# Attention and a dense block on one core: a list-scheduled order over named buffers, row-tiled scores, pooled V by matmul, q and k pooled before their transposes

## Chip, cores, metric

The kernel runs on one core of one Trainium2 chip. The metric is device time in microseconds (us), the median of several runs. The kernel before takes 449.98 us (median of 3 runs, 449.43 to 450.81).

Engine names as the profile has them: PE is TensorE, PEld its weight loads (these overlap PE), DVE VectorE, ACT ScalarE, POOL GpSimd, SP the queue that issues loads and stores.

## The reference

```python
# q, k, v: [8 batches, 8 heads, 576, 64]; w_in: [512, 2048]; w_out: [2048, 512]
q_d, k_d, v_d = (t.reshape(B, H, 144, 4, D).mean(axis=3) for t in (q, k, v))
out_d = softmax(scale * q_d @ k_d.T) @ v_d               # 144 pooled positions
out_up = np.repeat(out_d, 4, axis=2)
mask = np.abs(pos[:, None] - pos[None, :]) < 4           # a band of 7 keys
out_local = softmax(where(mask, scale * q @ k.T, -1e9)) @ v
x = (out_up + out_local) -> [4608, 512]                  # token major
h = x @ w_in
return (h - np.tanh(h)) @ w_out                          # [4608, 512]
```

There are two parts. Attention works on 32 pairs of heads, four pairs to a batch. The dense part, two matrix products, works on nine blocks of 512 tokens, and each block needs all four pairs of the batches that its tokens come from.

## The kernel before

A pair's q and k come in as tokens by features. DVE reorders them, PE transposes them into PSUM, ACT evicts them into `qk`. DVE then copies the keys into `kz`, whose other head's rows are zero, so that a full 128-row matmul gives the scores of one head. POOL pools q and k from the evicted transposes.

```python
def a_T(p):
    ...                                     # 9 transposes, 3 evictions to qk
    for hh in range(2):                     # zero-padded keys, one per head
        nc.vector.tensor_copy(out=kz[r, hh], in_=win)
    nc.gpsimd.tensor_tensor(out=tmp, in0=v2[:, :, :, 0], in1=v2[:, :, :, 1], op=ALU.add)
    nc.gpsimd.tensor_tensor(out=qd[:, 0], in0=t2[:, 0, :, 0], in1=t2[:, 0, :, 1], op=ALU.add)
    for hh in range(2):
        nc.gpsimd.tensor_tensor(out=kd[r, :, 64 * hh:64 * hh + 48], ...)
    nc.gpsimd.tensor_scalar_mul(qd[:, 1], qd[:, 0], 1.0 / 16.0)

def a_S(p, hh):                             # scores of one head
    for t in range(NT):
        nc.tensor.matmul(ps[...], kz[:, hh, t, :], qk[:, QW * t:QW * t + NQ[t]], ...)
    for i, m in enumerate(ms):
        nc.tensor.matmul(ps[...], kd[:, m, :], qd, ...)
    ...                                     # exp on ACT, mask on DVE
```

V is loaded twice: once in overlapping windows of 128 tokens (`vst`), once grouped by four tokens (`vg`), from which POOL pools it.

```python
def prep_v(hb):                             # four heads
    nc.gpsimd.tensor_copy(out=vw3[hb % 3][:, :, :, 0:64], in_=vst[hb])
    nc.gpsimd.tensor_tensor(out=tmp, in0=vg[:, :, :, 0:128], in1=vg[:, :, :, 128:256], op=ALU.add)
    for i in range(2):
        nc.gpsimd.tensor_tensor(out=vd[r, ...], in0=tmp[r, :, :, 0:64], in1=tmp[r, :, :, 64:128], op=ALU.add)
```

The order of the program is written by hand. `pump(n)` puts up to n quads (four matmuls of 128x512, 0.87 us) of dense work between the steps, if their batches are done.

```python
for p in range(NPAIR):
    ...                                     # loads
    a_T(p + 1); pump(1)
    a_O(p); pump(2)                         # outputs, normalisation
    a_S(p + 1, 0); pump(1)
    a_X(p); pump(1)                         # transpose back to xT
    a_S(p + 1, 1)
    a_reorder(p + 2); prep_v(...); load_v(...)
    pump(3)
while quads:
    quads.pop(0)[1]()                       # the dense work that is left
```

The softmax here doesn't subtract the row's maximum and nothing guards it: scores larger than these inputs give would overflow.

Of the kernel before, what the change touches and what calls it, by code (L numbers as in the profile page):

```python
# [10 lines left out]
ALU = mybir.AluOpType  # L11
PSUM = bass.MemoryType.PSUM


@with_exitstack
def kernel(
# [14 lines left out]
    NPAIR = B * NP  # L31
    G = S // 4
# [10 lines left out]
    work = ctx.enter_context(tc.tile_pool(name="work", bufs=2))  # L43
    moe = ctx.enter_context(tc.tile_pool(name="moe", bufs=2))
    ps_a = ctx.enter_context(tc.tile_pool(name="ps_a", bufs=1, space=PSUM))
    ps_m = ctx.enter_context(tc.tile_pool(name="ps_m", bufs=4, space=PSUM))

    def fixed(name, shape, dt):
        return const.tile(shape, dt, name=name, tag=name)

    ident = fixed("ident", [128, 128], BF16)
    mask = fixed("mask", [128, 576], BF16)
# [3 lines left out]
    qk2 = [fixed(f"qk{i}", [128, 1192], BF16) for i in range(2)]  # L56
    kz2 = [fixed(f"kz{i}", [128, 2, NT, 128], BF16) for i in range(2)]
    kd2 = [fixed(f"kd{i}", [128, 3, 128], BF16) for i in range(2)]
    vw3 = [fixed(f"vw{i}", [128, 4, NT, 65], BF16) for i in range(3)]
    vg2 = [fixed(f"vg{i}", [128, 2, 3, 256], FP32) for i in range(2)]  # L60
    vd3 = [fixed(f"vd{i}", [128, 2, 3, 130], BF16) for i in range(3)]


    def emit_ident():
        nc.gpsimd.memset(ident, 0.0)
        nc.gpsimd.affine_select(
            out=ident, in_=ident, compare_op=ALU.not_equal, fill=1.0,
            base=0, pattern=[[-1, 128]], channel_multiplier=1,
        )

    def emit_zeros(i):
        nc.vector.memset(qk2[i], 0.0)
        nc.vector.memset(kz2[i], 0.0)
        nc.vector.memset(kd2[i], 0.0)

    def emit_vzeros(i):
        if i < 2:
            nc.vector.memset(vg2[i], 0.0)
        nc.vector.memset(vd3[i], 0.0)
        nc.vector.memset(vd3[i][0:48, :, :, 64:65], 4.0)  # L80
        nc.vector.memset(vd3[i][64:112, :, :, 129:130], 4.0)
        nc.vector.memset(vw3[i][:, :, :, 64:65], 1.0)

    def emit_mask():

        nc.gpsimd.memset(mask, 1.0)
        m4 = mask[:, 0:480].rearrange("p (t c) -> p t c", c=QW)
        for part, pat in ((m4, [[0, 4], [1, QW]]),
                          (mask[:, 480:576], [[1, 96]])):
            neg = [[-s, n] for s, n in pat]  # L90
            nc.gpsimd.affine_select(
                out=part, in_=part, compare_op=ALU.is_ge, fill=0.0,
                base=-1, pattern=neg, channel_multiplier=1)
            nc.gpsimd.affine_select(
                out=part, in_=part, compare_op=ALU.is_ge, fill=0.0,
                base=7, pattern=pat, channel_multiplier=-1)
        nc.gpsimd.affine_select(
            out=mask[:, 0:QW], in_=mask[:, 0:QW], compare_op=ALU.is_ge,
            fill=0.0, base=-4, pattern=[[0, QW]], channel_multiplier=1)
        nc.gpsimd.affine_select(  # L100
# [4 lines left out]
    qkn, tails, vst = {}, {}, {}  # L105

    def load_qk(hb):
        b, h0 = hb // 2, 4 * (hb % 2)
        t = work.tile([128, 2, 4, 256], BF16, name="qkn", tag="qkn", bufs=3)
        qkn[hb] = t  # L110
        for i, src in enumerate((q, k)):
            nc.gpsimd.dma_start(
                out=t[:, i],
                in_=src[b, h0:h0 + 4, 0:512, :].rearrange(
                    "h (g a) d -> g h (a d)", a=4))
        if hb % 2 == 0:
            tl = work.tile([128, H * D], BF16, name="tl", tag="tl")
            tails[b] = tl
            for i, src in enumerate((q, k)):
                nc.gpsimd.dma_start(  # L120
                    out=tl[64 * i:64 * i + 64, :].rearrange(
                        "p (h d) -> p h d", d=D),
                    in_=src[b, :, 512:576, :].rearrange("h p d -> p h d"))

    def load_v(hb):
        b, h0 = hb // 2, 4 * (hb % 2)
        t = work.tile([128, 4, NT, 64], FP32, name="vst", tag="vst")
        vst[hb] = t
        for i in range(4):
            h = h0 + i  # L130
            base = v[b, h]

            def win(tok, n, nt):
                return bass.AP(tensor=base.tensor, offset=base.offset + tok * D,
                               ap=[[D, n], [QW * D, nt], [1, D]])
            if b == 0 and h == 0:
                nc.vector.memset(t[0:32, i, 0, :], 0.0)
                nc.sync.dma_start(out=t[4:128, i, 0, :], in_=v[b, h, 0:124, :])
                nc.sync.dma_start(out=t[:, i, 1:5, :], in_=win(QW - 4, 128, 4))
            elif b == B - 1 and h == H - 1:  # L140
                nc.vector.memset(t[96:128, i, 4, :], 0.0)
                nc.sync.dma_start(out=t[0:100, i, 4, :], in_=v[b, h, 476:576, :])
                nc.sync.dma_start(out=t[:, i, 0:4, :], in_=win(-4, 128, 4))
            else:
                nc.sync.dma_start(out=t[:, i], in_=win(-4, 128, 5))
        vg = vg2[hb % 2]
        for i in range(4):
            nc.sync.dma_start(
                out=vg[64 * (i % 2):64 * (i % 2) + 48, i // 2],
                in_=v[b, h0 + i].rearrange("(m g a) d -> g m (a d)", m=3, a=4))  # L150

    def prep_v(hb):
        nc.gpsimd.tensor_copy(out=vw3[hb % 3][:, :, :, 0:64], in_=vst[hb])
        vg, vd = vg2[hb % 2], vd3[hb % 3]
        tmp = work.tile([128, 2, 3, 128], FP32, name="vtmp", tag="vtmp", bufs=1)
        nc.gpsimd.tensor_tensor(out=tmp, in0=vg[:, :, :, 0:128],
                                in1=vg[:, :, :, 128:256], op=ALU.add)
        for i in range(2):
            r = slice(64 * i, 64 * i + 48)
            nc.gpsimd.tensor_tensor(  # L160
                out=vd[r, :, :, 65 * i:65 * i + 64], in0=tmp[r, :, :, 0:64],
                in1=tmp[r, :, :, 64:128], op=ALU.add)


    st = {}

    def a_reorder(p):
        src = qkn[p // 2]
        qr = work.tile([128, 2, 4, 128], BF16, name="qr", tag="qr")
        st[p] = {"qr": qr}  # L170
        h = 2 * (p % 2)
        for i in range(2):
            nc.vector.tensor_copy(  # L173
                out=qr[:, i].rearrange("p a (h d) -> p h a d", d=D),
                in_=src[:, i, h:h + 2, :].rearrange("p h (a d) -> p h a d", d=D))

    def a_T(p):
        qr, tl = st[p]["qr"], tails[p // 4]
        j = p % 4
        ps = ps_a.tile([128, 2, 1024], BF16, name="ps_t", tag="ts")  # L180
        for i in range(2):
            for a in range(4):
                nc.tensor.transpose(  # L183
                    ps[:, 0, 512 * i + 128 * a:512 * i + 128 * a + 128],
                    qr[:, i, a, :], ident)
        nc.tensor.transpose(ps[:, 1, 0:128], tl[:, 128 * j:128 * j + 128], ident)  # L186
        qk = qk2[p % 2]
        full = bass.AP(tensor=qk.tensor, offset=qk.offset,
                       ap=[qk.ap[0], [KOFF, 2], [1, 576]])
        for i in range(2):  # L190
            nc.scalar.copy(  # L191
                out=full[:, i, 0:512].rearrange("p (g a) -> p g a", a=4),
                in_=ps[:, 0, 512 * i:512 * i + 512].rearrange(
                    "p (a g) -> p g a", a=4))
        nc.scalar.copy(  # L195
            out=full[:, :, 512:576],
            in_=ps[:, 1, 0:128].rearrange("p (i c) -> p i c", i=2))

        kz = kz2[p % 2]
        for hh in range(2):  # L200
            r = slice(64 * hh, 64 * hh + 64)
            kk = qk[r, :]
            win = bass.AP(tensor=kk.tensor, offset=kk.offset + KOFF - 4,
                          ap=[kk.ap[0], [QW, NT], [1, 128]])
            nc.vector.tensor_copy(out=kz[r, hh], in_=win)  # L205

        tmp = work.tile([128, 2, 288], BF16, name="tmp", tag="tmp")
        v2 = full.rearrange("p i (g a) -> p i g a", a=2)
        qd = work.tile([128, 2, G], BF16, name="qd", tag="qd")
        with nc.allow_low_precision("pooled q and k"):  # L210
            nc.gpsimd.tensor_tensor(out=tmp, in0=v2[:, :, :, 0],  # L211
                                    in1=v2[:, :, :, 1], op=ALU.add)
            t2 = tmp.rearrange("p i (g a) -> p i g a", a=2)
            nc.gpsimd.tensor_tensor(out=qd[:, 0], in0=t2[:, 0, :, 0],  # L214
# [222 lines left out]
```

## Time and profile before

| what | value |
|---|---|
| time, span of the profiled run | 449.98 us, 448.2 us |
| PE, DVE, ACT, POOL busy | 77%, 61%, 46%, 50% |
| first dense matmul starts (timeline) | 72.9 us |
| last transpose back of attention starts | 371.7 us |
| from there to the end: dense work alone | 219 ns per matmul |

The page of the kernel before: the busy line, the span in 40 slices of 11.2 us (each digit tenths busy), and the chain of work that ended last.

```profile
span 448.2 us, 6961 instructions
PE 344.2 (77%) x2550; PEld 198.6 (44%) x2592; DVE 271.2 (61%) x486; ACT 206.8 (46%) x373; POOL 222.1 (50%) x293
...
PE   1034447864888888888888888888888889999996
...
DMA  9999998530563656484919290929023010101111
...
PE 47%; POOL 23%; DVE 15%; issue 6%; ACT 6%; DMA 2%; SPq 2%; POOLq 0%; ACTq 0%
```

PE is busy at most four tenths in the first six slices, some eight tenths in the body, and full at the end. POOL holds 23% of the chain though it is busy only half the time, so some of PE's waits are for it. The first six slices have the DMA engines at nine tenths.

The timeline of the kernel before, a piece of the start (start us, duration us, engine, line, operation; in brackets the idle time before it and what ended it):

```profile
53.04 1.15 POOL L211 TENSOR_TENSOR tmp<-qk_79 128x576 bf16<-128x576 bf16 x1 [3.31 <-ACT qk_79 L195]
53.53 0.66 PE L231 MATMUL ps_s_436<-qk_79,kz_81 128*128 128x120 bf16 x5 [0.83 <-DVE kz_81 L205]
54.27 0.42 POOL L214 TENSOR_TENSOR qd<-tmp 128x144 bf16<-128x144 bf16 x1
54.65 0.91 POOL L220 TENSOR_TENSOR kd_83<-tmp 64x144 bf16<-64x144 bf16 x2
...
55.66 0.56 POOL L223 TENSOR_SCALAR qd<-qd 128x144 bf16<-128x144 bf16 x1
56.27 0.40 PE L236 MATMUL ps_s_436<-qd,kd_83 128*128 128x144 bf16 x2 [2.08 <-POOL qd L223]
...
61.85 1.03 PE L183 MATMUL ps_t<-ident,qr 128*128 128x128 bf16 x8 [3.44 <-DVE qr L173]
```

The pooled scores (L236) wait 2.08 us for four POOL operations that could begin only when the transposes were evicted; the next pair's transposes start 8.3 us after the first scores. In the body the same waits recur, 1.3 us each, and a pair takes 11 us.

### The profile page before, as it was taken

What the parts mean: (1) busy time and instruction counts of PE and PEld (TensorE: products, weight loads), DVE (VectorE), ACT (ScalarE), POOL (GpSimd) and SP (SyncE); (2) the same over time, 40 slices, a digit from 0 to 9 for tenths busy, and PEclk for the clock granted to TensorE, in tenths of its full rate; (3) what the DMA queues carried; (4) which work ended last, traced back from release to release, by engine and by line L of the source; (5) the groups of instructions that cost most, each with busy time, mean ns of one, the idle gap of its engine ahead of it and who ended that gap; (6) DMA issues with size and microseconds to landing.
All of it is one profiled execution on the core that took longest, in us unless ns stands there. A gap on an engine that the chain in (4) does not pass through costs nothing.

```text
span 448.2 us, 6961 instructions
## 1 busy us (share of the span) xinstructions
PE 344.2 (77%) x2550; PEld 198.6 (44%) x2592; DVE 271.2 (61%) x486; ACT 206.8 (46%) x373; POOL 222.1 (50%) x293
## 2 busy tenths in 40 slices
PE   1034447864888888888888888888888889999996
PEld 0023335543545454545454444545454554444442
DVE  6025464966676777777777767676767665343420
ACT  1122224752455555555555555555555543444421
POOL 7478686646665755666465747574727220000000
PEclk9999999985799999999999999999999999999999
DMA  9999998530563656484919290929023010101111
GB/s 126 213 193 198 169 200 104 112 48 0 60 141 66 147 73 131 77 160 57 171 35 177 41 182 26 179 40 181 25 75 95 22 41 25 47 25 47 44 52 70
DMA packets 86993, 43.44 MB, mean 97 GB/s; under 512 B 52655, under 2 KB 82351, under 8 KB 86959
## 3 DMA queue, kind: packets, MB, share of 16 engines
q1 hardware_dynamic: 57390, 29.36, 27.4%
q0 software_dynamic: 29568, 13.64, 24.4%
q8 instruction: 20, 0.33, 0.3%
q14 instruction: 15, 0.11, 0.1%
HBM read 47.18 MB, written 9.44 MB: 126 GB/s over the span
## 4 chain that ended last, share of the span: by engine, by line
PE 47%; POOL 23%; DVE 15%; issue 6%; ACT 6%; DMA 2%; SPq 2%; POOLq 0%; ACTq 0%
PE ps_h L308 17%; PE ps_y L322 17%; DVE E L244 9%; POOL tmp L211 8%; PE ps_t L183 4%; POOL qd L223 4%; ACT E L242 4%; POOL qd L214 3%; POOL kd_82 L220 3%; POOL kd_83 L220 3%; PE ps_o L262 2%; PE ps_o L255 2%; DMA vg_87<-in_v_dram 2%; DVE gT L313 1%; DVE qr L173 1%
## 5 line engine op out<-in xcount | busy, mean ns | idle before, releaser
L322 PE MATMUL ps_y<-w_out_sb,gT 128*128 128x512 bf16 x547 | 139.5, 379 | 1.5
L312 ACT ACTIVATE u<-ps_h 128x512 f32<-128x512 f32 x144 | 86.1, 598 | 101.9 <-PE ps_h L308 100.8
L313 DVE TENSOR_TENSOR gT<-ps_h,u 128x512 bf16<-128x512 f32 x144 | 98.6, 687 | 50.0 <-ACT u L312 49.2
L244 DVE TENSOR_TENSOR E<-E,mask 128x576 bf16<-128x576 bf16 x64 | 59.4, 928 | 49.5 <-ACT E L242 49.4
L308 PEld LDWEIGHTS <-w_in_sb 128*128 128x128 bf16 x576 | 54.4, 99 | 55.9 <-issue 2.2
L322 PEld LDWEIGHTS <-gT 128*128 128x128 bf16 x576 | 53.7, 98 | 51.5
L211 POOL TENSOR_TENSOR tmp<-qk_79 128x576 bf16<-128x576 bf16 x16 | 18.3, 1146 | 78.6 <-PE ps_o L262 60.7
L308 PE MATMUL ps_h<-xT_74,w_in_sb 128*128 128x512 bf16 x144 | 55.3, 384 | 0.1
L308 PE MATMUL ps_h<-xT_73,w_in_sb 128*128 128x512 bf16 x142 | 54.5, 384 | 0.9 <-issue 0.4
L308 PE MATMUL ps_h<-xT_75,w_in_sb 128*128 128x512 bf16 x143 | 54.9, 384 | 0.0
L308 PE MATMUL ps_h<-xT_72,w_in_sb 128*128 128x512 bf16 x134 | 51.1, 382 | 0.1
L183 PE MATMUL ps_t<-ident,qr 128*128 128x128 bf16 x256 | 23.0, 242 | 32.8 <-DVE qr L173 32.8
L211 POOL TENSOR_TENSOR tmp<-qk_78 128x576 bf16<-128x576 bf16 x16 | 18.3, 1144 | 40.7 <-PE ps_o L262 31.9
L183 PEld LDWEIGHTS <-qr 128*128 128x128 bf16 x256 | 18.0, 108 | 43.0 <-DVE qr L173 40.1
L205 DVE COPY kz_81<-qk_79 64x640 bf16<-64x640 bf16 x32 | 15.5, 486 | 27.7 <-ACT qk_79 L195 27.2
L205 DVE COPY kz_80<-qk_78 64x640 bf16<-64x640 bf16 x32 | 15.5, 485 | 26.6 <-ACT qk_78 L195 26.1
L327 ACT COPY y<-ps_y 128x512 f32<-128x512 f32 x36 | 21.1, 585 | 20.0 <-PE ps_y L322 20.0
L191 ACT COPY qk_78<-ps_t 128x512 bf16<-128x512 bf16 x32 | 17.2, 591 | 24.9 <-PE ps_t L186 24.9
L269 DVE TENSOR_TENSOR ln<-ps_o,r 128x640 bf16<-128x640 f32 x32 | 26.4, 824 | 1.1
L191 ACT COPY qk_79<-ps_t 128x512 bf16<-128x512 bf16 x32 | 17.2, 591 | 8.1 <-PE ps_t L186 8.1
L236 PEld LDWEIGHTS <-kd_82 128*128 128x128 bf16 x48 | 4.9, 102 | 35.6 <-POOL kd_82 L220 26.6
L223 POOL TENSOR_SCALAR qd<-qd 128x144 bf16<-128x144 bf16 x32 | 18.1, 566 | 2.9
(272 smaller groups left out, 514.2 us busy)
## 6 DMA issues: line engine op xcount, KB each, us to landing
vst<-in_v_dram SPq DMA_DIRECT2D x62, 160.0 KB, 3.3
out_dram<-y SPq DMA_DIRECT2D x36, 256.0 KB, 2.0
vg_87<-in_v_dram SPq DMA_DIRECT2D x32, 144.0 KB, 4.2
vg_88<-in_v_dram SPq DMA_DIRECT2D x32, 144.0 KB, 4.3
qkn<-in_q_dram POOLq DMA_DIRECT2D x16, 256.0 KB, 4.8
qkn<-in_k_dram POOLq DMA_DIRECT2D x16, 256.0 KB, 5.6
w_in_sb<-in_moe_w_in_dram POOLq DMA_DIRECT2D x4, 512.0 KB, 8.4
w_out_sb<-in_moe_w_out_dram POOLq DMA_DIRECT2D x4, 512.0 KB, 8.5
```

Of the source, the lines that this page charges most:

```text
L183: nc.tensor.transpose(ps[:, 0, 512 * i + 128 * a:512 * i + 128 * a + 128], qr[:, i, a, :], ident)
L191: nc.scalar.copy(out=full[:, i, 0:512].rearrange("p (g a) -> p g a", a=4), in_=ps[:, 0, 512 * i:512 * i + 512].rearrange("p (a g) -> p g a ...
L205: nc.vector.tensor_copy(out=kz[r, hh], in_=win)
L211: nc.gpsimd.tensor_tensor(out=tmp, in0=v2[:, :, :, 0], in1=v2[:, :, :, 1], op=ALU.add)
L220: nc.gpsimd.tensor_tensor(out=kd[r, :, 64 * hh:64 * hh + 48], in0=t3[:, :, :, 0], in1=t3[:, :, :, 1], op=ALU.add)
L223: nc.gpsimd.tensor_scalar_mul(qd[:, 1], qd[:, 0], 1.0 / 16.0)
L244: nc.vector.tensor_tensor(out=E[:, hh, 0:576], in0=E[:, hh, 0:576], in1=mask, op=ALU.mult)
L269: nc.vector.tensor_tensor(out=ln[:, 0:5, :].rearrange("p t (h d) -> p h t d", d=D), in0=blocks[:, :, 0:5, 0:64], in1=r[:, :, 0:5].unsqueez ...
L308: nc.tensor.matmul(ps, w_in_sb[:, dc, fc * 128:(fc + 1) * 128], xT[dc][:, kb * 512:kb * 512 + 512], start=(dc == 0), stop=(dc == N_DC - 1))
L312: nc.scalar.activation(out=u, in_=ps, func=AF.Tanh)
L313: nc.vector.tensor_tensor(out=gTs[kb][:, fc, :], in0=ps, in1=u, op=ALU.subtract)
L322: nc.tensor.matmul(ps, gTs[kb][:, fc, ts * 128:ts * 128 + 128], w_out_sb[:, fc, :], start=(fc == 0), stop=(fc == N_FF - 1))
```

## The change

There are four parts. (1) The hand-written order goes. Each step is given to a small list scheduler with its engine, an assumed duration in ns, the names of the buffers it reads and writes, and a priority; it simulates the engines and emits in order of start. (2) Scores are row-tiled: the two heads sit in rows 0 to 63 and 64 to 127, each matmul uses its 64 rows, and the `kz` copies go. (3) V is loaded once, and six matmuls with a 0/1 matrix sum its groups of four. (4) q and k are pooled on POOL before the transposes, straight from the loaded layout, and matmuls with the identity transpose the sums. The first pairs also alternate between two sets of PSUM banks.

The diff holds smaller changes too. The main ones: q and k are loaded by pair (128 KB a load) and no longer by four heads (256 KB). The scores of a pair come in two groups over both heads, and only the second holds pooled scores; before, the first head's group held some already and waited for them. The exps, the masks and the normalisation are regrouped to match: masks of 960 and 192 columns for two of 576, one normalisation of 896 for 640 and 256. And the second product of the first dense block follows its first product at once, so that 32 quads and not 16 can be done before the second batch is.

```diff
+class Program:
+    def op(self, eng, ns, fn, reads=(), writes=(), pri=0): ...   # dependencies by name
+    def order(self): ...          # list schedule: earliest engine, lowest priority
 ...
-            nc.vector.tensor_copy(out=kz[r, hh], in_=win)
 ...
+        def score(t, hh, c):
+            rows = slice(64 * hh, 64 * hh + 64)
+            k0 = KOFF + QW * t - 4
+            T.matmul(sc[:, c:c + NQ[t]], qk[s][rows, k0:k0 + 128],
+                     qk[s][rows, QW * t:QW * t + NQ[t]], start=True, stop=True)
 ...
+            for t in range(NT):                                  # pooled V
+                T.matmul(pv[:, 0, :], pick[:, t, :], vw[w][:, :, t, 0:64],
+                         start=(t == 0), stop=(t == NT - 1))
 ...
+                GP.tensor_tensor(out=sm1, in0=src[:, :, :, 0:128],
+                                 in1=src[:, :, :, 128:256], op=ALU.add)
 ...
+        if p < NP and p % 2 == 1:
+            ps, po, ts, ox = ps_ts1, ps_ox1, ["ts1"], ["ox1"]
 ...
-    for p in range(NPAIR):
-        ...  a_T, pump, a_O, pump, a_S, ...
+    P.emit()
```

## The prediction

> **What bounds the kernel now** (span 448.2 us). Two things, in turn.
> (1) Start: the timeline shows the first dense matmul at 72.9 us. Until then pairs of heads run one after another, PE under 5 of each 10 us. The chain of waits runs through POOL: V pooling until 22 us, then per pair tmp 1.15, qd 0.43, kd 0.91, qd 0.57 us while the scores wait.
> (2) 110 to 370 us: one pair per 11 us (21.95 us per two, by the starts of tmp in the chain), PE busy 83 to 87%. The order is fixed: eight dense quads (4 matmuls of 128x512, 0.87 us) per pair, and waits for qd recur (1.3 us). The remaining dense work runs alone from 370 us at 219 ns per matmul, PE 99% busy.
>
> PE's own work by instruction starts: dense 1152 x 0.219 = 252 us, attention about 2.25 us per pair. From 72.9 us that is 252 + 28 x 2.25 = 315 us, but the last matmul ends at 444.5: 57 us of gaps.
>
> **What changes, per pair (estimates from durations in the trace).**
> - POOL: tmp/qd/kd (3.0 us) and half of V's cast, vtmp and vd (2.6) become two adds (1.6) and a cast (0.65). POOL leaves the chain; half-size loads add 0.8 us of issue.
> - DVE: two kz copies (0.97 us) go; kd out of PSUM (0.27) comes. Masks: 0.66 + 0.26 us uncontended (576 columns took 459 ns median, 928 mean, up to 2.1 us beside POOL's adds and casts).
> - ACT: qd (0.28) and a V eviction (0.25) are added; about 4.0 us.
> - PE: pooling transposes and V matmuls add 0.5 us; row tiling saves 0.3 if the two heads' scores overlap. The Trainium skill, "TensorEngine Tiling (Array Packing)", Key Properties, says changing tiling mode drains TensorE; four changes per pair, which no run here shows yet. I count 2.5 us plus drains.
> - DMA: the second V load (9.4 MB) goes. This matters only in the first 63 us, where the queues are saturated (near 200 GB/s).
>
> **Where it counts.** Pooled q/k no longer wait for evicted transposes, and early pairs alternate between two PSUM sets. Chain per pair: transposes 0.9, evictions 1.7, scores and exps 2.8, output to xT 4 us, two deep. I expect the first dense matmul at 43 us (gain 30), limited by loads and POOL's order.
> After it PE-bound: 252 + 28 x 2.5 = 322 us. The emitted order has about 6 quads per pair, and stretches around pairs 7-8 and 11-12 with no dense work left, where PE must wait. With these, drains, and DVE and ACT over 80% busy I add 25 us of gaps. The end (copy, store) is 3.7 us as now; timing is 1.8 us above the span.
> 43 + 322 + 25 + 5.5 = 395; attention started before 43 us gives back 4.
>
> **Predicted: 391 us, 80% range 375 to 409. Faster 0.97, same 0.02, slower 0.01.**
>
> **What would show it.** First dense matmul at 38 to 48 us; PE over 88% busy from there; attention over by 275 us, then dense alone for 105 us; POOL busy about 140 us and out of the chain; the two heads' score matmuls starting within a few ns.
>
> **What would make it wrong.** w_out late (saturated queues until 65 us) with PE's order fixed; drains over 0.2 us each; a static order built on durations shorter than measured (tanh 598 ns, subtract 687 ns), so that PE stalls each pair; masks still blocked by POOL.

## The result, and the profile after

The changed kernel is correct and takes 393.9 us (median of 4 runs, 393.53 to 394.27); the kernel before took 450.01 us in the same rounds. The ratio is 0.8752, with a 95% interval of 0.8736 to 0.8768. A ratio here is the mean time of one kernel's runs over that of the other's of the same rounds, so not quite the ratio of the medians quoted. Executions over 1.5% slower than the fastest of the same kernel are left out of the means.

The page of the changed kernel, the same lines (slices of 9.8 us):

```profile
span 392.6 us, 7296 instructions
PE 348.9 (89%) x2835; PEld 191.5 (49%) x2880; DVE 228.9 (58%) x417; ACT 221.8 (56%) x421; POOL 151.0 (38%) x203
...
PE   1466798976996899999999999999999999999996
...
PEclk9997599998999799999999999999999999999999
DMA  9699993466759648568554400000010010101012
...
PE 80%; ACT 8%; DVE 8%; issue 2%; DMA 2%; POOL 1%; ACTq 0%; DVEq 0%; POOLq 0%
```

PE does the same amount of busy time, 349 against 344 us, in a span that is 56 us shorter. POOL has left the chain. The granted clock (PEclk) dips in the fourth, fifth, tenth and fourteenth slices, in which PE was six to eight tenths busy. The first dense matmul starts at 43.1 us (before 72.9), the last transpose back at 287.6 us (before 371.7), and dense work is alone for 101 us at the end. PE's remaining idle time sits early, as the windows of the changed kernel show (stretch: its length, then busy us of each engine, the granted PE clock, the DMA share and GB/s):

```profile
42.90:100.00 57.10, 48.39 (x384) 25.71 (x390) 31.32 (x58) 31.95 (x60) 31.15 (x39) 0.93 0.76 122
100.00:150.00 50.00, 44.94 (x475) 28.12 (x481) 40.45 (x77) 36.19 (x74) 34.78 (x45) 0.93 0.65 106
150.00:288.00 138.00, 135.57 (x1306) 77.20 (x1327) 99.59 (x184) 97.11 (x191) 49.55 (x62) 1.00 0.37 71
288.00:388.90 100.90, 100.36 (x458) 45.49 (x465) 35.93 (x52) 39.53 (x68) 0.00 (x0) 1.00 0.11 42
```

From 43 to 388.9 us PE is idle for 16.7 us of 346, and 13.8 us of that lie before 150 us. The kernel before had lost much more in the same parts; its windows:

```profile
72.90:110.00 37.10, 26.33 (x217) 16.65 (x218) 28.16 (x51) 19.50 (x37) 22.79 (x29) 0.83 0.35 53
110.00:150.00 40.00, 32.88 (x261) 19.82 (x267) 27.05 (x48) 20.86 (x38) 24.51 (x31) 0.90 0.47 80
150.00:370.00 220.00, 187.32 (x1525) 108.86 (x1549) 157.76 (x282) 120.47 (x220) 123.01 (x160) 1.00 0.50 98
370.00:444.60 74.60, 74.08 (x344) 33.73 (x348) 25.96 (x38) 28.27 (x49) 0.00 (x0) 1.00 0.11 43
```

So the 56 us are two things: about 30 us of an earlier start, and the 51 us of idle PE after it cut to 17. PE's own work rose a little (320.6 to 329.3 us busy), which takes 9 us back.

### The profile page after: what moved, and what is told of

Same layout as the page of the kernel before. It is cut to its first block, busy times and chain, and to the rows that moved or that the text cites. A ratio compares the mean times of both kernels' runs of the same rounds, so it can differ in the third digit from the quotient of the medians.

```text
span 392.6 us, 7296 instructions
## 1 busy us (share of the span) xinstructions
PE 348.9 (89%) x2835; PEld 191.5 (49%) x2880; DVE 228.9 (58%) x417; ACT 221.8 (56%) x421; POOL 151.0 (38%) x203
## 4 chain that ended last, share of the span: by engine, by line
PE 80%; ACT 8%; DVE 8%; issue 2%; DMA 2%; POOL 1%; ACTq 0%; DVEq 0%; POOLq 0%
PE ps_hy_497 L499 8%; PE ps_hy_498 L524 8%; PE ps_hy_499 L499 8%; PE ps_hy_499 L524 8%; PE ps_hy_500 L499 8%; PE ps_hy_500 L524 7%; PE ps_hy_497 L524 7%; PE ps_hy_498 L499 7%; PE ps_ts L397 3%; PE ps_ts L363 3%; PE ps_ox L444 2%; PE ps_ox L312 2%; ACT qk_89 L377 2%; ACT qk_90 L377 2%; PE ps_ox L474 2%
## 5 line engine op out<-in xcount | busy, mean ns | idle before, releaser
L524 PEld LDWEIGHTS <-gT_103 128*128 128x128 bf16 x320 | 29.2, 97 | 32.7
L524 PEld LDWEIGHTS <-gT_104 128*128 128x128 bf16 x256 | 24.0, 98 | 27.1
L377 ACT COPY qk_89<-ps_ts 128x512 bf16<-128x512 bf16 x32 | 17.7, 591 | 25.6 <-PE ps_ts L369 24.6
L377 ACT COPY qk_90<-ps_ts 128x512 bf16<-128x512 bf16 x28 | 15.5, 590 | 15.8 <-PE ps_ts L369 14.1
L524 PE MATMUL ps_hy_498<-w_out_sb,gT_103 128*128 128x512 bf16 x79 | 20.0, 379 | 0.0
L524 PE MATMUL ps_hy_500<-w_out_sb,gT_103 128*128 128x512 bf16 x78 | 19.6, 379 | 0.4 <-issue 0.3
L524 PE MATMUL ps_hy_497<-w_out_sb,gT_103 128*128 128x512 bf16 x75 | 19.5, 379 | 0.3
L524 PE MATMUL ps_hy_499<-w_out_sb,gT_103 128*128 128x512 bf16 x76 | 19.4, 379 | 0.2
L347 POOL TENSOR_TENSOR sm_88<-half 128x256 bf16<-128x256 bf16 x16 | 11.2, 701 | 19.8 <-PE ps_ts L369 18.8
L347 POOL TENSOR_TENSOR sm_87<-half 128x256 bf16<-128x256 bf16 x16 | 12.0, 747 | 17.8 <-PE ps_ts L369 16.8
L363 PE MATMUL ps_ts<-ident,qr_84 128*128 128x128 bf16 x128 | 11.0, 234 | 7.6 <-DVE qr_84 L335 6.7
L460 DVE TENSOR_TENSOR ln_99<-ps_ox,r_97 128x896 bf16<-128x896 f32 x16 | 17.4, 1086 | 0.3
L416 ACT ACTIVATE E_95<-ps_ts 128x960 bf16<-128x960 f32 x16 | 15.6, 976 | 3.4 <-PE ps_ts L397 3.4
L420 DVE TENSOR_TENSOR E_95<-E_95,mask 128x960 bf16<-128x960 bf16 x16 | 12.4, 776 | 8.2 <-ACT E_95 L416 8.0
L416 ACT ACTIVATE E_96<-ps_ts 128x960 bf16<-128x960 f32 x14 | 13.6, 974 | 6.1 <-PE ps_ts L397 6.1
L397 PE MATMUL ps_ts<-qk_89 64*128 64x120 bf16 (+1 forms) x160 | 9.9, 219 | 7.7 <-ACT qd_91 L387 4.5
L524 PE MATMUL ps_hy_500<-w_out_sb,gT_104 128*128 128x512 bf16 x61 | 15.8, 379 | 0.4 <-issue 0.2
L524 PE MATMUL ps_hy_498<-w_out_sb,gT_104 128*128 128x512 bf16 x62 | 16.0, 379 | 0.1
L524 PE MATMUL ps_hy_497<-w_out_sb,gT_104 128*128 128x512 bf16 x61 | 15.9, 379 | 0.1
L524 PE MATMUL ps_hy_499<-w_out_sb,gT_104 128*128 128x512 bf16 x60 | 15.6, 379 | 0.3 <-issue 0.3
L460 DVE TENSOR_TENSOR ln_100<-ps_ox,r_98 128x896 bf16<-128x896 f32 x14 | 15.2, 1087 | 0.3
## 6 DMA issues: line engine op xcount, KB each, us to landing
w_out_sb<-in_moe_w_out_dram POOLq DMA_DIRECT2D x4, 512.0 KB, 12.5
```

The lines of the kernel that those rows point to most:

```text
L347: GP.tensor_tensor(out=sm[s].rearrange("p i (h d) -> p i h d", d=D), in0=sm1[:, :, :, 0:64], in1=sm1[:, :, :, 64:128], op=ALU.add)
L363: T.transpose(b16[:, c:c + 128], qr[s][:, i, a, :], ident)
L377: op("ACT", 480, lambda i=i: A.copy(out=full[:, i, 0:512].rearrange("p (g a) -> p g a", a=4), in_=b16[:, 512 * i:512 * i + 512].rearrange( ...
L397: T.matmul(sc[:, c:c + NQ[t]], qk[s][rows, k0:k0 + 128], qk[s][rows, QW * t:QW * t + NQ[t]], start=True, stop=True)
L416: op("ACT", 870, lambda: A.activation(out=E[s][:, 0:960].rearrange("p (h c) -> p h c", h=2), in_=ps[:, :, 0:480], func=AF.Exp, scale=SCALE ...
L420: op("DVE", 760, lambda: V.tensor_tensor(out=E[s][:, 0:960].rearrange("p (h c) -> p h c", h=2), in0=E[s][:, 0:960].rearrange("p (h c) -> p ...
```

## Experiments

The total came out near the prediction, so the question was whether for its reasons. Four parts changed together; the runs take them apart. All twelve were correct. The kernel before ran beside them at a median of 450.4 to 450.6 us on their chips, so that times can be set beside the 393.9 us; a difference of 1 us or less is not read. Each kernel is a patch on the changed one, and the scheduler reorders the rest after each patch, unless the order is said to be fixed: an "undo" measures a part together with the new order it leads to.

### Order against operations

**hand_order**: the new operations, emitted in the old loop's order.

```diff
-    P.emit()
+    for p in range(NPAIR):            # the old loop, over groups of the new steps
+        ...; put("T", p + 1); pump(1)
+        if p % 2 == 0: put("poolv", p // 2)
+        put("O", p); pump(2); put("S1", p + 1); pump(1); put("X", p); pump(1); put("S2", p + 1)
+        ...; pump(3)
```

> New operations, old hand-written order (eight dense quads per pair, one pair ahead); the list schedule is dropped. Theory A (the new operations, which take POOL out of the chain, are most of the gain; any order that keeps PE fed does): 392 to 410 us, pair period about 9.4 us while dense work lasts. Rival B (the list schedule is most of the gain): 425 us or more.

Measured: 433.55 us (433.38 to 433.94), ratio 0.9631, by its number in the range of rival B. The waits of PE in hand_order (us in total, times, longest us) show that the largest was my own making:

```profile
PE ps_ox L457 <- ACT vd L326: 21.1, 16, 1.9
PE ps_ts L373 <- DVE qr L344: 17.6, 8, 6.7
PE ps_ts L377 <- POOL sm L356: 9.6, 1, 9.6
```

The outputs (L457) wait for ACT's eviction of the pooled V, because the V pooling matmuls stood right before them. The old order had no place for this new step, and I had chosen a bad one.

**hand_order_early_v** moves them ahead of the next pair's transposes.

```diff
+        if p % 2 == 0: put("poolv", p // 2)
         put("T", p + 1); pump(1)
-        if p % 2 == 0: put("poolv", p // 2)
```

> The first hand-ordered kernel, with the V pooling matmuls moved ahead of the next pair's transposes: in the first one PE waited 21.1 us (16 times) for their eviction just before the output matmuls, a cost of where they were placed. If that is a real cost of the placement: 410 to 416 us, so that new operations in the old order are worth about 38 us and the list schedule the other 18 us. If the list schedule is most of the gain whatever the placement (rival B): 425 us or more.

Measured: 414.52 us (412.88 to 415.72), ratio 0.9205. This is in the range expected: one misplaced step had cost 19 us. The first dense matmul is at 58.8 us, the last transpose back at 328.6 us.

**old_ops_listed**: the old operations (V pooling on POOL from a second load, q and k pooled after the evictions, zero-padded keys), ordered by the list scheduler. It is the three undos below in one kernel.

> Old operations (q/k pooled on POOL after the transposes, V pooled on POOL from a second load, zero-padded full-array scores) in the list schedule with two PSUM sets for the first batch. Theory A: 410 to 432 us, first dense matmul at 58 us or later, POOL back in the waits of PE. Rival B: under 402 us.

Measured: 419.5 us (418.92 to 419.86), ratio 0.9315, in theory A's range. POOL is busy 256 us and holds 14% of the chain; but the first dense matmul is at 46.6 us, where theory A had 58 us or later, and the last transpose back is at 347.1 us.

| | old operations | new operations |
|---|---|---|
| hand-written order | 450.5 us, dense from 72.9 us | 414.5 us, dense from 58.8 us |
| list-scheduled order | 419.5 us, dense from 46.6 us | 393.9 us, dense from 43.1 us |

Read along the sides, the order is worth 31 us with the old operations and 21 with the new ones, the operations 36 us in the hand-written order and 26 in the listed one, both together 56.5. One reserve: the upper left cell is the kernel before itself, and the other three cells share the smaller changes named with the diff. The two differences that leave that cell out are clean of them, 21 us for the order (against this one hand-written order) and 26 us for the operations. The other 10 us or so are the smaller changes and what the parts do to one another; the runs don't divide them. Of the earlier start, 15.7 us are the order's (58.8 to 43.1) and 3.5 us the operations' in the listed order (46.6 to 43.1); how much of the rest the smaller loads and the regrouped scores bring is not shown.

**one_psum_set** takes the second set of PSUM banks away from the first pairs.

```diff
-        if p < NP and p % 2 == 1:
-            ps, po, ts, ox = ps_ts1, ps_ox1, ["ts1"], ["ox1"]
```

> Changed kernel, but all pairs of the first batch use one PSUM set. If the second set is what shortened the start (rival C): first dense matmul at 52 us or later and 402 us or more. Theory A (start set by loads, POOL's order and DVE, as the trace shows pair 2 waiting for its reordered q/k and not for PSUM): first dense 44 to 49 us, 395 to 400 us.

Measured: 394.13 us (392.62 to 395.34), ratio 0.8751 (0.8719 to 0.8783); first dense matmul at 44.0 us; the time is just under theory A's range. The second set is worth nothing that shows in this kernel.

**measured_ns** gives the scheduler the durations that the trace shows in place of the assumed ones, which are mostly shorter (tanh 600 for 490, reorder 400 for 240, and so on for 20 steps).

```diff
-        op("ACT", 490, lambda: A.activation(out=u[us], in_=ps_hy[slot], func=AF.Tanh),
+        op("ACT", 600, lambda: A.activation(out=u[us], in_=ps_hy[slot], func=AF.Tanh),
```

> Changed kernel with the scheduler's durations set to those measured in its trace (tanh 600, subtract 690, evictions 590, exp 970 and 810, ln 1090 ns and so on). If the gaps of 24 us after the first dense matmul come from an order built on short durations (rival D): 374 to 384 us. Theory A (gaps sit between 60 and 135 us, where the dense work released by finished batches runs out, and in cold clock): 388 to 395 us.

Measured: 404.85 us (403.24 to 405.31), ratio 0.8984, outside both ranges. The better durations gave a schedule 11 us worse: the last transpose back is at 300.3 us, and PE waits 14.1 us in 21 waits for the normalised outputs. Why this order is worse was not tested. It shows that putting the measured durations in is no remedy by itself, and that the result of such a scheduler moves by several per cent with its inputs: no operation changed here, and the time moved by 11 us. The undos below let the scheduler reorder as well, and no run undoes a part with the order held fixed, so a cost of 11 us or less there can't be told from that of another order.

### The operations one by one

**undo_tiling** puts the zero-padded keys back.

```diff
+            op("DVE", 485, pad, reads=[("qk", s, 1), ("qk", s, 2)], writes=[("kz", s, hh)], pri=pri)
 ...
-            T.matmul(sc[:, c:c + NQ[t]], qk[s][rows, k0:k0 + 128],
-                     qk[s][rows, QW * t:QW * t + NQ[t]], start=True, stop=True)
+            T.matmul(sc[:, c:c + NQ[t]], kz[s][:, hh, t, :],
+                     qk[s][:, QW * t:QW * t + NQ[t]], start=True, stop=True)
```

> Changed kernel, list schedule kept, scores again as full-array matmuls on zero-padded keys: two key copies on DVE (0.97 us) and one more pooled-key copy (0.31 us) per pair, PE about 0.15 us more per pair in the score matmuls. If only the PE time counts: 397 to 400 us. If the key copies lengthen the chain and load DVE so that PE stalls (theory E gives it a smaller part than q/k pooling): 400 to 407 us.

Measured: 420.28 us (419.12 to 422.0), ratio 0.9348, so 26.4 us slower, far outside both ranges: the largest single part. It is not for PE's sake. The timeline of the changed kernel around one row-tiled group of scores:

```profile
181.00 1.03 PE L524 MATMUL ps_hy_499<-w_out_sb,gT_103 128*128 128x512 bf16 x4
181.96 0.39 PE L397 MATMUL ps_ts<-qk_90 64*128 64x120 bf16 x8
182.28 0.39 PE L499 MATMUL ps_hy_498<-xT_65,w_in_sb 128*128 128x512 bf16 x1
```

and of undo_tiling around a zero-padded one:

```profile
187.83 0.59 PE L510 MATMUL ps_hy<-xT,w_in_sb 128*128 128x512 bf16 x2
188.26 0.58 PE L409 MATMUL ps_ts<-qk,kz 128*128 128x120 bf16 x8
188.68 1.67 PE L510 MATMUL ps_hy<-xT,w_in_sb 128*128 128x512 bf16 x7
```

From the start of the eight score matmuls to the next start it is 0.32 us tiled and 0.42 us padded. But the four dense matmuls before the tiled group take 0.96 us to its start, where four at 0.215 us would take 0.86: a gap of 0.1 us, and the padded group has none (0.43 us for two). This fits the Trainium skill, "TensorEngine Tiling (Array Packing)", Key Properties: changing the tiling mode drains TensorE. The records of the single matmuls, which the timeline merges, show it at both ends (medians after 150 us): 0.311 us from the last dense start to a tiled group against 0.216 us to a padded one, and 0.145 us from the last of the eight score starts to the next dense one against 0.053 us. Within a tiled group the two heads' matmuls start 4 ns apart. So over a pair's two groups tiling saves some 0.35 us (first start to last: 0.17 and 0.12 us for 0.37 and 0.27) and pays four drains of some 0.09 us, which leaves PE with nothing. What undo_tiling does show is PE waiting for DVE (us in total, times, longest):

```profile
PE ps_ox L481 <- DVE ln L471: 12.2, 10, 2.2
PE ps_ox L313 <- DVE xT L490: 9.5, 6, 1.9
...
PE ps_ts L409 <- DVE kz L401: 6.6, 7, 2.8
```

That left two readings. Either DVE, with 31 us more of copies, is late with everything, or the copies hurt because the scores wait for them.

**extra_key_copies** keeps the row tiling and makes DVE do the two key copies per pair into a buffer that nothing reads.

```diff
+            def pad(hh=hh, rh=rh):
+                V.tensor_copy(out=kz[s][rh, hh], in_=...)      # kz is never read
+            op("DVE", 485, pad, reads=[("qk", s, 1), ("qk", s, 2)], writes=[("kz", s, hh)], pri=pri)
```

> The changed kernel, row tiling kept, plus the two zero-padded key copies per pair on VectorE, written where nothing reads them. Putting the untiled scores back cost 26.4 us (420.3 against 393.9 us). Theory A (load: VectorE's extra 2 x 32 copies of 0.49 us, 31 us in all, delay its other work, the layer norms and scores, whoever reads the copies): 410 to 422 us, VectorE busy near 260 us, TensorE waiting for VectorE's layer-norm work. Theory B (chain: the copies hurt because the scores wait for them): 393 to 401 us.

Measured: 398.43 us (397.53 to 400.15), ratio 0.8861, in theory B's range. The busy line of its page:

```profile
PE 354.4 (89%) x2880; PEld 193.1 (49%) x2880; DVE 254.4 (64%) x481; ACT 222.3 (56%) x421; POOL 150.4 (38%) x203
```

DVE is busy 254.4 us (228.9 in the changed kernel, 264.4 in undo_tiling), but the time rises by only 4.5 us. DVE's load is a small part, and some 22 of the 26 us are left for what undo_tiling has besides: scores that wait for a copy, padded copies of the pooled keys (two short ones for one), and the order that follows. So the same copies, with what goes with them, cost far more in the chain of each pair than beside it. The wait for `kz` itself is only 6.6 us; that the rest shows up in the later waits for `ln` and `xT`, behind it in the same pair's chain, is argued and not tested.

**undo_v** puts back the second load of V and its pooling on POOL.

```diff
+                nc.sync.dma_start(out=vg[hb % 2][:, 0, i], in_=v[b, h0 + i, 0:512, :]...)
-            for t in range(NT):
-                T.matmul(pv[:, 0, :], pick[:, t, :], vw[w][:, :, t, 0:64], ...)
+            GP.tensor_tensor(out=vtmp[r, c], in0=g[r, c, :, 0:128], in1=g[r, c, :, 128:256], op=ALU.add)
+            GP.tensor_tensor(out=vd[w][r, c, :, 0:64], in0=vtmp[r, c, :, 0:64], in1=vtmp[r, c, :, 64:128], op=ALU.add)
```

> Changed kernel, list schedule kept, V alone pooled on POOL from a second load again. The three old operations together cost 25.6 us in the list schedule. If POOL's added time (about 3.9 us per two pairs) and its place before the first output matter most: 402 to 410 us. If POOL off the pair's chain costs nothing in the steady state: 394 to 399 us.

Measured: 410.38 us (408.29 to 413.72), ratio 0.9122, 16.5 us slower and just above the higher range, with POOL busy 217 us for 151.

**extra_v_load** keeps the matmul pooling and adds only the second load, landed and not read.

```diff
+                nc.sync.dma_start(out=vg[hb % 2][:, 0, i], in_=v[b, h0 + i, 0:512, :]...)
+    load_vg(0); load_vg(1)
```

> The changed kernel plus the second load of V (9.4 MB more, in the layout that the old pooling wanted), landed and not read. Putting the old V pooling back cost 16.5 us (410.4 us). If the bytes cost the time: 404 to 412 us, the first dense matmul later than 43 us. If the pooling work on POOL and what waits for it cost the time (my theory): 393 to 397 us.

Measured: 410.12 us (408.73 to 415.64; the slowest of the four is left out of the ratio), ratio 0.91. My theory fell. The 9.4 MB that nobody reads cost as much as the whole old V pooling. That does not make the 66 us of POOL work free: undo_v has them in place of the V pooling matmuls (six of 0.67 us together per four heads, some 11 us of PE's time in all) and of sixteen evictions on ACT of 0.59 us, and its masks on DVE take 54.4 us against 35.1 us here. What the two runs show is that, beside the same load, the two ways to pool V come out even, so that the part's gain goes with the load. The windows of extra_v_load (columns as before):

```profile
43.00:65.00 22.00, 14.49 (x67) 6.50 (x68) 8.59 (x15) 8.06 (x15) 12.12 (x16) 0.73 1.29 189
65.00:100.00 35.00, 28.86 (x246) 15.35 (x245) 14.46 (x31) 18.31 (x34) 14.46 (x18) 0.98 0.53 102
100.00:150.00 50.00, 41.03 (x400) 25.57 (x397) 35.88 (x65) 31.81 (x63) 27.85 (x35) 0.86 0.70 135
```

The windows of the changed kernel for the same stretches:

```profile
43.00:65.00 22.00, 19.92 (x132) 9.84 (x134) 14.52 (x24) 15.05 (x28) 14.04 (x18) 0.89 1.12 167
65.00:100.00 35.00, 28.47 (x252) 15.87 (x256) 16.70 (x34) 16.90 (x33) 17.11 (x21) 0.95 0.53 94
100.00:150.00 50.00, 44.94 (x475) 28.12 (x481) 40.45 (x77) 36.19 (x74) 34.78 (x45) 0.93 0.65 106
```

The loss is in the start, while the DMA is full: 67 matmuls against 132 in 43 to 65 us, and by 150 us PE has done 12 us less of busy work. The first dense matmul is only 2.3 us later (45.4 us). What is late are the inputs of the second batch. Its first reorders start at 50.3, 52.2 and 72.7 us, against 40.9, 43.0 and 58.5 us, and the timeline has PE standing 5.64 us, until 60.49 us, for POOL's sums of q and k. POOL starts these only at 58.5 us, after it has stood 3.6, 2.3 and 1.8 us for loads of w_out to land before it issues further loads (at 45.8 us in the changed kernel). A w_in load takes 12.9 us from issue to landing (median) against 8.9 us, one of w_out 17.0 against 12.5. The Trainium skill, "DMA: Bandwidth & Descriptors", Queues, rings and completion order, says that each DMA engine takes turns between the queues that have work for it; that agrees with V, on the SP queue, slowing q, k and weights, on POOL's queue. One reserve: the scheduler knows of the added load too and emits another order in the start, so how much of the 16 us is bytes and how much is that order stays open. That the way of pooling is not the cause stands on undo_v and extra_v_load being equal.

**undo_qk** pools q and k on POOL after the evictions, as before.

```diff
-        op("POOL", 1100, add1, reads=[("qkn", sn, jj, 0), ("qkn", sn, jj, 1)], ...)
-                T.matmul(g32[:, G * i:G * i + 128], sm[s][:, i, :], ident, ...)
+        op("POOL", 1150, ... tmp ..., reads=[("qk", s, i) for i in range(3)], ...)
+        ...                                # qp, kd, qd on POOL
```

> Changed kernel, list schedule kept, q/k alone pooled on POOL from the transposed layout again: about 2.6 us of POOL work between the evictions and the second half of the scores of each pair. Theory E (this chain is the largest part of the 25.6 us): 404 to 412 us. If the list schedule hides the longer chain behind dense work: 394 to 399 us.

Measured: 401.74 us (399.38 to 402.28), ratio 0.8913, 7.8 us slower, between the two ranges, and the first dense matmul at 39.2 us, earlier than with the part. The part saves the later waits for POOL's qd (9.7 us in seven waits in undo_qk) and nothing of the start; at 7.8 us it is within what another order alone can cost.

The three undos cost 26.4, 16.5 and 7.8 us, 51 in sum; undone together (old_ops_listed) they cost 25.6. They are not additive. That they lengthen branches that run beside one another, so that one hides behind another, would explain it, and so would the orders that the scheduler found; which it is was not tested.

### What is left

PE's idle in the changed kernel lies at 60 to 65, 80 to 95 and 120 to 130 us. Until the second batch is done there are only the 32 quads of the first block, and they run out early. For the last stretch the emitted order has more to say: dense quads stop at the fifty-second and go on when the third batch is done, because the second product of the second block had been held back to be interleaved with the third block.

**dense_blocks** emits that second product right after its first.

```diff
-        if kb == 0 or kb == 1:
+        if kb <= 2:
             for i in range(16):
                 mm1(kb, i)
-            if kb == 0:
+            if kb < 2:
                 for i in range(16):
                     mm2(kb, i)
             return
```

(The expectations count blocks and batches from 0 in part: their batch 2 is the third.)

> The changed kernel with the second dense block's second product emitted right after its first one, not held until batch 2 is done, so that there are 16 more blocks of dense work to fill TensorE before the attention of batch 2 is finished. If the idle of TensorE at 110 to 135 us and the lower clock after it come from dense work having run out (my theory): 386 to 391 us and the stretch 100 to 150 us with more TensorE work than 44.9 us. If that idle comes from attention's own chain, or the dense work put there is only missed later: 393 to 395 us.

Measured: 389.18 us (387.13 to 389.75), ratio 0.8631 (0.8608 to 0.8654), as expected and better than both kernels. The windows of dense_blocks:

```profile
65.00:100.00 35.00, 28.55 (x275) 16.46 (x276) 15.56 (x31) 16.77 (x33) 15.26 (x20) 0.95 0.50 90
100.00:150.00 50.00, 49.43 (x494) 28.44 (x494) 39.32 (x74) 36.56 (x73) 33.47 (x41) 1.00 0.73 132
```

The stretch from 100 to 150 us has 49.4 us of PE work for 44.9, at a full clock. The stretch before it, 6.5 us idle, is as it was.

**dense_blocks_late_w** moves the load of w_out behind more loads of q, k and V as well.

```diff
-    W_IN_PRI, W_OUT_PRI = -25, 0
+    W_IN_PRI, W_OUT_PRI = -25, 10
```

> As dense_blocks, and the load of w_out moved behind the loads of q, k and v for more pairs. If the idle at 60 to 95 us comes from inputs of the next pairs that stand behind the weights in the DMA queues: 2 to 5 us less than dense_blocks. If it comes from the length of a batch's attention chain, or the second products now wait for w_out: no gain, or up to 5 us more than dense_blocks.

Measured: 393.5 us (391.28 to 394.85), ratio 0.8735: 4 us worse than dense_blocks, and PE is busy 27.3 us of the 35 from 65 to 100 us, less than the 28.6 there. The idle of 60 to 95 us is not mended by moving w_out back. What bounds it, the chain of a batch or other loads, stays open.

## Why the prediction was right, and where not

- **Total.** 391 us predicted, 393.9 measured.
- **Start.** Predicted at 43 us, measured at 43.1. The reasons given were partly wrong. The step "early pairs alternate between two PSUM sets" is worth nothing (44.0 us without), and "pooled q/k no longer wait for evicted transposes" is not what brought the start forward (39.2 us without it). With the old operations the listed order starts dense work at 46.6 us; of the 30 us, 15.7 are shown to be the order's, and the smaller loads and regrouped scores stand untested. A right number for partly wrong reasons is partly luck.
- **After the start.** 322 us of work and 25 us of gaps, less 4 us given back, make 343; measured are 345.7 us from 43.1 to 388.8, of which 329 busy and 17 idle. The work was put too low by 7 and the gaps too high by 8; that these cancel is luck. Most of the 7 need not be more work: PE was busy 12.6 us at half clock after 43.1 us, which at full clock would have taken some 6 us less (an estimate from the trace's clock record, by halving). "PE over 88% busy" held: 95%. The gaps where no dense work is left were foreseen, and dense_blocks confirmed one of them.
- **Attention over by 275 us, then 105 us of dense work.** Measured 287.6 and 101 us: attention was slower, while dense work filled its gaps better.
- **Row tiling.** The prediction listed it as a saving of 0.3 us per pair on PE. The matmuls do save 0.35 us, and "the two heads' score matmuls starting within a few ns" held (4 ns); but four drains of 0.09 us (within the bound of 0.2 each that was set) take it back. It is nevertheless the largest part, 26 us; what the runs point to is that it takes the key copies out of each pair's chain. The prediction counted the copies as 0.97 us of DVE time; as mere DVE time they cost 4.5 us (extra_key_copies). How much of the 26 us is the order that came with them is open.
- **Second V load.** "This matters only in the first 63 us" was right about where, but no term of the sum carried it: adding the load costs 16 us, with the reserve made above. The POOL work that the prediction counted (2.6 us per pair on average) came out even with the matmuls and evictions that replaced it.
- **POOL.** About 140 us and out of the chain predicted; 151 us and 1% of the chain.
- **Masks.** 0.66 and 0.26 us were predicted uncontended; the trace has means of 0.75 and 0.34 us, less than the 2 x 0.93 before. The groups of the kernel before (busy us in all, mean ns | idle before):

```profile
L244 DVE TENSOR_TENSOR E<-E,mask 128x576 bf16<-128x576 bf16 x64 | 59.4, 928 | 49.5 <-ACT E L242 49.4
```

The groups of the changed kernel, for its two E buffers:

```profile
L420 DVE TENSOR_TENSOR E_95<-E_95,mask 128x960 bf16<-128x960 bf16 x16 | 12.4, 776 | 8.2 <-ACT E_95 L416 8.0
L420 DVE TENSOR_TENSOR E_96<-E_96,mask 128x960 bf16<-128x960 bf16 x16 | 11.7, 728 | 5.3 <-ACT E_96 L416 5.1
L433 DVE TENSOR_TENSOR E_95<-E_95,mask 128x192 bf16<-128x192 bf16 x16 | 6.7, 416 | 11.3 <-ACT E_95 L427 11.2
L433 DVE TENSOR_TENSOR E_96<-E_96,mask 128x192 bf16<-128x192 bf16 x16 | 4.1, 256 | 3.9 <-ACT E_96 L427 3.8
```

  The Trainium skill, "SBUF — State Buffer", Who interferes with whom, says that a DVE instruction with two SBUF inputs contends with a POOL instruction that reads SBUF. The trace agrees: before, the same multiplication took 459 ns in the median and 2.1 us at 209.60 us, beside a POOL addition from 209.59 us.
- **"A static order built on durations shorter than measured, so that PE stalls."** Not borne out: with the measured durations it was 11 us slower. That tries one other order and does not show that short durations are good.
- **"w_out late".** It was not: the fourth load was issued at 41.2 us and no load of it took over 13.0 us, its first use came at 65.4 us, and PE has no wait for it.

The total was right because its two sizes, the start and PE's work with a few gaps, were right; how the parts share in it was not known from the trace alone, and the runs settle it only in part.

## What to carry to other kernels

Cost an operation by whether the next step of the same chain waits for it: 31 us of copies beside the chain cost 4.5 us here, the same copies inside it, with what goes with them, 26. While the DMA queues were full here, bytes that nobody needed delayed bytes that were needed now (as far as the reserve above allows), so count a removed load there even if nobody waits for it. When parts are undone one at a time their costs need not add up (51 against 26 us), so run the whole of the old operations under the new order too, hold the order fixed at least once, and treat the order as a variable of its own, as worth trying as any operation.

## What the Trainium skill lacked or had wrong

- "TensorEngine Tiling (Array Packing)", Key Properties, names the drain at a change of tiling mode but has no figure: here 0.095 us per change from dense matmuls to 64-row score matmuls and 0.092 us back.
- "TensorE: Matmul & The Clock Gate", Part 3, Measured speedup vs the span model, has no row for two 64-row tiles: eight matmuls of 120 columns took 0.17 us from first to last start tiled and 0.37 us full, a factor of two without the drains; with the drain at the end it is 0.32 against 0.42 us to the next start.
- The same page, Part 1, The HAM clock gate, puts the halved clock after at least one idle window of about 3.4 us. The trace has it after less: the clock record of the changed kernel is at half from 34.1 to 47.8 us (`--windows` gives 0.50, and 1.00 for 30.7 to 34.1 us), and PE's one wait in the 3.4 us before is of 1.92 us, its longest in the 20 us before of 2.28 us. The first dense matmuls are 0.43 us apart from 43.9 us on (timeline below), against 0.215 us at full clock. Idle PE is thus paid twice; the two stretches before 150 us were granted 0.93 of the clock.

```profile
43.90 0.63 PE L499 MATMUL ps_hy_497<-xT_67,w_in_sb 128*128 128x512 bf16 x1 [0.22 <-issue]
44.33 0.63 PE L499 MATMUL ps_hy_497<-xT_68,w_in_sb 128*128 128x512 bf16 x1
44.76 0.63 PE L499 MATMUL ps_hy_498<-xT_65,w_in_sb 128*128 128x512 bf16 x1
```

- I found no page with a figure for what a load that nobody waits for costs the others: 9.4 MB more, unread, cost 16 us (with the reserve made above), and a 512 KB load of w_in landed 12.9 in place of 8.9 us after issue.
